# Late stages of a fused attention and gated-MLP gradient kernel: DMAs issued in program order, transposed w_down loaded in chunks, first operands of the next stage loaded into dead buffers

## The chip, the core and the metric

The kernel runs on one core of a Trainium2 chip. The core has five engines with a queue of instructions each: TensorE (PE, matmuls; its weight loads are listed apart as PEld), VectorE (DVE), ScalarE (ACT), GpSimd (POOL) and SyncE (SP). An engine works through its queue in order, and an instruction starts when the semaphores that it waits for have come. DMAs are issued by POOL (plain copies, queue q0 of the profile) and by SP (here mostly DMAs that transpose, queue q1); 16 DMA engines carry them out. SBUF is the working memory, PSUM takes the sums of the matmuls.

The metric is the device time of one execution in microseconds (us), as the median of several runs. Smaller is better.

## What is computed

The kernel computes a block and all its gradients for a given grad_out. S = 2048 rows, D = 576, H = 32 heads of 128, F = 4608, everything in bfloat16:

```python
def _fwd_reference(A_x, A_k_cache, A_v_cache, A_wq, A_wo, B_x, B_w_gate, B_w_up, B_w_down):
    def _A_ref(x, k_cache, v_cache, wq, wo):
        ...
        scores = jnp.einsum("bhqd,bhkd->bhqk", q, k_cache) * (Dh ** -0.5)
        p = _softmax(scores, axis=-1)
        o = jnp.einsum("bhqk,bhkd->bhqd", p, v_cache)
        return (lambda x, *d: x.transpose(*d))(o, 0, 2, 1, 3).reshape(B, Sq, H * Dh) @ wo
    def _B_ref(x, w_gate, w_up, w_down):
        g = jnp.einsum("bsd,df->bsf", x, w_gate)
        u = jnp.einsum("bsd,df->bsf", x, w_up)
        h = _sigmoid(g) * u
        return jnp.einsum("bsf,fd->bsd", h, w_down)
    x = A_x
    xn = _layernorm(x, axis=-1)
    s = _A_ref(xn, A_k_cache, A_v_cache, A_wq, A_wo)
    g = _silu(_B_ref(xn, B_w_gate, B_w_up, B_w_down))
    return x + s * g
```

The outputs are this value (out_0) and the gradients of x (out_1), of the k and v caches (out_2, out_3), of wq (out_4), wo (out_5), w_gate, w_up and w_down (out_6 to out_8).

## The kernel before

The kernel has a forward MLP pass, the attention with its gradients, and then four late stages, which the change touches. A row tile is 128 of the 2048 rows, so there are 16 (`NT`); `DT` = 5 tiles cover the 576 columns and `FT` = 36 the 4608. Some results go through DRAM between stages (names ending in `_d`).

- The forward pass (to about 540 us) ends with loop L403 to L439. For each row tile it computes the MLP's output, and DVE makes from it g2 (the silu), ds_t (grad_out times g2) and dsil, the derivative of silu (L433). g2, dsil and ds_t are stored.
- The attention (to about 3711 us) works head by head and leaves in DRAM `on2_d`, the heads' outputs (shown as on_d), and `dq2_d`, the gradients of the queries (shown as dq_d).
- **Stage A** (L760 to L829): s = o @ wo, row tile by row tile. For each tile, a transposing DMA (`load_oT`, L469) brings the tile's 32 heads into one of two buffers, KQ and oTb, in turn; 32 heads in two column pieces make 64 matmuls (L813). The rows of wo lie in dead buffers of the attention (dsT, Kn, Vn, dOn), except the last six heads, which come in `wo_x`. DVE then makes doB = s * dsil * grad_out (L819, L820), the gradient at the MLP's output, and o0 = s * g2 + x (L822, L823) from loads of two tiles each (L797 to L803, one buffer each). doB is transposed on PE (L58). In the same loop stand loads for stage B: the whole of w_down transposed (wdT_sb, ten pieces, L786), xn_all (L790) and the first blocks of a and h (L792, L793).
- **Stage B** (L854 to L893): 18 blocks of 256 columns of F. A block has 80 matmuls for dh = doB @ w_down^T (L872), DVE and ACT make du and dg of it (L873 to L877), and 3 x 64 matmuls (L842) make the weight gradients. Those of w_up and w_gate are transposed by SP (L892) before they are stored (L850, L852).
- **Stage C** (L908 to L931): for each head 32 matmuls for the gradient of wo (onb by ds_all) and 32 for that of wq (dqb by xn_all). onb and dqb come for four heads at a time (L916, L917), in two buffers each. The gradient of wq leaves through dqT (two buffers, L925) and a transposing DMA by SP (L926). The loop also loads w_up and w_gate transposed, ten pieces (L928 and L63, into wuT_sb and wgT_sb).
- **Stage D** (L938 to L1010): the gradient of the normed x for 8 blocks of 256 rows, each the sum over 36 + 36 + 32 tiles of du @ w_up^T, dg @ w_gate^T and dq @ w_q^T, 416 matmuls (L964). The left operands come as transposed chunks by SP (cu, cg, cq, L955); w_q^T is loaded in five pieces in the first blocks (L957).

What sets the order: the program is written for a framework that puts the instructions of each engine in an order of its own, by its estimate of when they can start, and derives every wait from the tiles that an instruction reads and writes. So a load in the text of stage A can be issued before or after others of the same engine. The late pools are opened by

```python
    def late(name, bufs=1, **kw):
        return tc.tile_pool(name=name, bufs=bufs, reuse_waits="tile", **kw)
```

which makes a new tile wait only for the tiles whose memory it takes.

Of the kernel before, what the change touches and what calls it, by code (L numbers as in the profile page):

```python
# [9 lines left out]
bf = mybir.dt.bfloat16  # L10
# [3 lines left out]
P = 128  # L14
# [52 lines left out]
def kernel(  # L67
# [36 lines left out]
    dsil_d = dram.tile([S, D], bf, name="dsil_d")  # L104
# [126 lines left out]
    with tc.tile_pool(name="pa", bufs=1) as pa:  # L231
# [166 lines left out]
        with tc.tile_pool(name="a2h", bufs=3) as hp, \  # L398
# [4 lines left out]
            for sg in range(NT // SG):  # L403
# [4 lines left out]
                dsil = sb.tile([P, SG, D], bf, name="dsil")  # L408
                g2b = sb.tile([P, SG, D], bf, name="g2b")
                ds_t = sb.tile([P, SG, D], bf, name="ds_t")  # L410
                for sl in range(SG):
# [21 lines left out]
                    nc.vector.tensor_tensor(dsil[:, sl, :], sig[:], t1[:], op=ALU.subtract)  # L433
# [4 lines left out]
                nc.gpsimd.dma_start(dsil_d[grows, :].rearrange("(t p) d -> p t d", p=P), dsil[:])  # L438
# [307 lines left out]
    with late("pc") as pc:  # L746
        xn_all = pc.tile([P, NT, D], bf, name="xn_all")
        pc2 = tc.alloc_tile_pool(name="pc2", bufs=1, reuse_waits="tile")
# [3 lines left out]
        pcw = tc.alloc_tile_pool(name="pcw", bufs=1, reuse_waits="tile")  # L752
        wdT_sb = pcw.tile([P, DT, F], bf, name="wdT_sb")
        pcf = tc.alloc_tile_pool(name="pcf", bufs=1, reuse_waits="tile")
        ah_first = [pcf.tile([P, NT, FB], bf, name=nm) for nm in ("a_first", "h_first")]

        def load_blk(dst, src_d, fb):
            nc.gpsimd.dma_start(dst[:], src_d[:, fb * FB:(fb + 1) * FB].rearrange("(t p) f -> p t f", p=P))

        with late("c1w") as wp, late("c1b") as blk, late("c1l3") as ldp3, late("c1s", 2) as sb, \  # L760
# [14 lines left out]
            WH = ldiv(FT, 2) * P if FT % 2 else F // 2  # L775
            wd_pieces = [(i, r0) for i in range(DT) for r0 in range(0, F, WH)]
            NWD = -(-len(wd_pieces) // max(1, NT - 5))
            pend_tr = []
            for st in range(NT):
                if st + 1 < NT:  # L780
                    load_oT(oTs[(st + 1) % 2], st + 1)
                for _ in range(NWD if st else 0):
                    if wd_pieces:
                        i, r0 = wd_pieces.pop(0)
                        d0 = min(i * P, D - P)
                        nc.sync.dma_start_transpose(wdT_sb[:, i, r0:r0 + WH], B_w_down[r0:r0 + WH, d0:d0 + P])  # L786
                        if not wd_pieces:
                            zlow(wdT_sb)
# [5 lines left out]
                if st % SG1 == 0:  # L794
                    grows = slice(st * P, (st + SG1) * P)
                    g2b = ldp3.tile([P, SG1, D], bf, name="g2b")
                    nc.gpsimd.dma_start(g2b[:], g2_d[grows, :].rearrange("(t p) d -> p t d", p=P))  # L797
                    dsb = ldp3.tile([P, SG1, D], bf, name="dsb")
                    nc.gpsimd.dma_start(dsb[:], dsil_d[grows, :].rearrange("(t p) d -> p t d", p=P))
                    xb = ldp3.tile([P, SG1, D], bf, name="xb")  # L800
                    nc.gpsimd.dma_start(xb[:], x2[grows, :].rearrange("(t p) d -> p t d", p=P))
                    gob = ldp3.tile([P, SG1, D], bf, name="gob")
                    nc.gpsimd.dma_start(gob[:], go2[grows, :].rearrange("(t p) d -> p t d", p=P))  # L803
                    o0b = ldp3.tile([P, SG1, D], bf, name="o0b")
# [19 lines left out]
                if sl == SG1 - 1:  # L824
                    nc.gpsimd.dma_start(o0[grows, :].rearrange("(t p) d -> p t d", p=P), o0b[:])
# [216 lines left out]
```

## Time and profile before

| what | value |
|---|---|
| median of 3 runs | 5245.4 us (5234.62 to 5245.75) |
| the profiled execution's own time | 5251.32 us |
| its span in the trace | 5249.3 us |
| stage A: first matmul, next stage's first | 3720.9, 3916.4 us |
| stage B: first use of xn_all on PE | 3935.5 us |
| stage B to C: last matmul ends, next starts | 4502.0, 4535.5 us |
| stage D: first matmul, ACT starts on the last sum | 4811.7, 5239.4 us |
| L433, dsil: 16 DVE instructions | 749 ns each |
| cu chunks (768 KB), issue to landing | 5.4 us median, 9.0 at most |
| dwT transposes of stage B (L892), issue to landing | 2.4 us (dwg), 6.7 us (dwu) median |

How to read the views: a row of the timeline has the start, the duration in the queue or on the engine, the engine, the line, the operation and out<-in; in square brackets stands how long the engine had been idle before it and what ended that. In the view of waits, "PE acc L842 <- DMA onb<-on_d" means that the matmul of line 842 that writes acc waited for the DMA that loads onb. In the list of DMA issues, the last number is the median time from issue to landing. SPq and POOLq are the issuing queues of those engines. A DMA share of 1 means that the 16 DMA engines were busy all the time on average; more than 1 comes from transfers that overlap on an engine.

### The profile page before, as it was taken

The numbers are of one execution on the slowest core, as the hardware profiler recorded it, in microseconds if no ns is written. First come the engines' busy times: TensorE is split into PE (matmuls) and PEld (weight loads), VectorE is DVE, ScalarE is ACT, GpSimd is POOL, SyncE is SP. The second block draws the span as 40 slices with busy tenths as digits, with TensorE's granted clock in tenths as the row PEclk, the third lists the DMA queues.
The fourth block names the chain that finished last, engine by engine and source line by source line (L and its number), as shares of the span: only waits on it lengthen the run. The fifth ranks groups of instructions, "written<-read, shape, count | busy, mean of one in ns | idle before, by whom it ended". The sixth has DMA issues, their size and how long they took to land.

```text
span 5249.3 us, 127878 instructions
## 1 busy us (share of the span) xinstructions
PE 4959.8 (94%) x53585; PEld 3490.0 (66%) x54480; DVE 2580.0 (49%) x6718; ACT 2600.7 (50%) x4663; POOL 901.3 (17%) x1373
## 2 busy tenths in 40 slices
PE   7899999999999999999999999999689999598999
PEld 3345677777787787777777777777446666354454
DVE  4523566566566666666666666666234444000111
ACT  6421666666676676666666666666113333111000
POOL 1112211111111111111111111111122222111000
PEclk9999999999999999999999999999899999899999
DMA  7647999999999999999999999999976665977775
GB/s 269 228 159 176 188 208 209 206 210 204 193 211 216 201 211 205 202 209 212 201 203 196 210 207 210 209 202 215 218 175 190 179 181 169 220 191 168 157 150 109
DMA packets 2756448, 1033.71 MB, mean 197 GB/s; under 512 B 2662737, under 2 KB 2666962, under 8 KB 2755858
## 3 DMA queue, kind: packets, MB, share of 16 engines
q1 hardware_dynamic: 2658338, 699.96, 72.5%
q0 software_dynamic: 97520, 325.41, 19.3%
q8 instruction: 428, 7.01, 0.6%
q14 instruction: 162, 1.33, 0.1%
HBM read 177.67 MB, written 182.13 MB: 69 GB/s over the span
## 4 chain that ended last, share of the span: by engine, by line
PE 79%; issue 7%; DMA 6%; SPq 3%; DVE 2%; POOL 1%; ACT 1%; POOLq 0%; DVEq 0%; ACTq 0%
PE acc L622 15%; PE acc L563 14%; PE acc L842 12%; PE acc L964 7%; PE sp L516 7%; PE dp L586 5%; PE acc L212 5%; PE dh L872 3%; PE acct L145 2%; PE u_ps L365 2%; PE g_ps L363 2%; PE acc L425 2%; SPq L63 2%; DMA out_dram<-kvo 2%; PE acc L813 1%
## 5 line engine op out<-in xcount | busy, mean ns | idle before, releaser
L534 ACT ACTIVATE Pq<-sp 128x1024 bf16<-128x1024 f32 x1024 | 1048.0, 1024 | 318.5 <-PE sp L516 204.9
L622 PEld LDWEIGHTS <-Pq 128*128 128x128 bf16 x16384 | 1006.1, 98 | 242.3 <-issue 4.4
L593 ACT ACTIVATE t<-dp,negdelta 128x1024 bf16<-128x1024 f32 x512 | 571.6, 1116 | 222.1 <-PE dp L586 168.7
L589 DVE SCALAR_TENSOR_TENSOR Pq<-dp,negdelta,Pq 128x1024 bf16<-128x1024 f32 x512 | 655.6, 1280 | 43.7 <-PE acc L563 40.8
L563 PEld LDWEIGHTS <-PT 128*128 128x128 bf16 x8192 | 502.9, 98 | 129.3 <-DMA PT<-Pq 7.6
L586 PE MATMUL dp<-VT,dOT 128*128 128x512 bf16 x1728 | 543.9, 381 | 35.4 <-DVE Pq L589 35.1
L563 PE MATMUL acc<-Vn,PT 128*128 128x128 bf16 x8192 | 547.7, 219 | 14.0 <-DMA PT<-Pq 7.1
L563 PE MATMUL acc<-Kn,dST 128*128 128x128 bf16 x8192 | 552.1, 219 | 8.2 <-DMA dST<-Pq 4.7
L622 PE MATMUL acc<-dOn,Pq 128*128 128x128 bf16 x8192 | 546.9, 219 | 10.1
L516 PE MATMUL sp<-KQ 128*128 128x512 bf16 x1762 | 548.4, 380 | 2.8 <-ACT Pq L534 2.7
L622 PE MATMUL acc<-Qn,Pq 128*128 128x128 bf16 x8192 | 544.3, 220 | 3.4
L563 PEld LDWEIGHTS <-dST 128*128 128x128 bf16 x8192 | 493.1, 98 | 67.3 <-DMA dST<-Pq 6.6
L594 DVE TENSOR_TENSOR Pq<-t,Pq 128x1024 bf16<-128x1024 bf16 x512 | 354.3, 692 | 357.1 <-ACT t L593 350.4
L980 DVE SCALAR_TENSOR_TENSOR junk<-dxn,xn_all 128x576 f32<-128x576 f32 x16 | 12.1, 758 | 711.9 <-ACT dxn L975 711.9
L603 ACT ACTIVATE dq_n<-acc,rsc 128x128 bf16<-128x128 f32 x512 | 188.3, 368 | 338.3 <-PE acc L563 338.3
L636 POOL DMA_DIRECT2D out_dram<-kvo x256 | 140.2, 548 | 1042.0 <-DVE kvo L634 1036.7
L557 POOL DMA_DIRECT2D on_d<-o_n x128 | 97.0, 758 | 742.7 <-DVE junk L575 392.1
L975 ACT ACTIVATE dxn<-acc 128x512 f32<-128x512 f32 (+1 forms) x32 | 12.8, 407 | 414.7 <-issue 310.1
L363 PE MATMUL g_ps<-wg_sb,xnT 128*128 128x512 bf16 x695 | 184.2, 388 | 28.8 <-DMA wg_sb<-in_B_w_gate_dram 15.0
L634 DVE SCALAR_TENSOR_TENSOR kvo<-acc,part 128x512 bf16<-128x512 f32 x256 | 176.1, 688 | 70.3 <-DMA out_dram<-kvo 35.4
L586 PEld LDWEIGHTS <-dOT 128*128 128x128 bf16 x2048 | 164.0, 98 | 63.2 <-issue 41.1
L50 DVE TENSOR_SCALAR o_n<-acc,rinv_all 128x128 bf16<-128x128 f32 x352 | 123.4, 351 | 168.2 <-PE acc L563 168.2
(199 smaller groups left out, 6842.6 us busy)
## 6 DMA issues: line engine op xcount, KB each, us to landing
out_dram<-kvo POOLq DMA_DIRECT2D x256, 128.0 KB, 4.2
h_d<-h_row POOLq DMA_DIRECT2D x48, 384.0 KB, 2.9
a_d<-a_row POOLq DMA_DIRECT2D x48, 384.0 KB, 2.8
du_d<-du_blk POOLq DMA_DIRECT2D x18, 1024.0 KB, 5.5
dg_d<-dg_blk POOLq DMA_DIRECT2D x18, 1024.0 KB, 7.8
x_all<-in_A_k_cache_dram SPq DMA_DIRECT2D x64, 256.0 KB, 5.6
on_d<-o_n POOLq DMA_DIRECT2D x128, 128.0 KB, 4.1
dq_d<-dq_n POOLq DMA_DIRECT2D x128, 128.0 KB, 3.8
```

The source lines that it names most:

```text
L212: nc.tensor.matmul(av[:, :CH], lhsT=w[:, i, :], rhs=srcT[:, i, cs], start=(i == 0), stop=(i == DT - 1))
L363: nc.tensor.matmul(g_ps[:], lhsT=xnT[:, i, srows], rhs=wg_sb[:, i, fs], start=(i == 0), stop=(i == DT - 1))
L516: nc.tensor.matmul(sp[:, c * CH:(c + 1) * CH], lhsT=hs.QT[:, qt * P:(qt + 1) * P], rhs=hs.KT[:, hf * HW_ + c * CH: hf * HW_ + (c + 1) * CH ...
L534: nc.scalar.activation(Pq[:, hsl], sp[:], AF.Exp, scale=SCALE, accum_out=hs.rsp[:, hf:hf + 1])
L563: nc.tensor.matmul(hs.acc[:, 0, :], lhsT=T[:, kt, :], rhs=rhs[:, kt, :], start=(kt == 0), stop=(kt == NT - 1))
L586: nc.tensor.matmul(dp[:, c * CH:(c + 1) * CH], lhsT=hs.dOT[:, qt * P:(qt + 1) * P], rhs=hs.VT[:, hf * HW_ + c * CH: hf * HW_ + (c + 1) * C ...
L589: nc.vector.scalar_tensor_tensor(Pq[:, hsl], dp[:], hs.negdelta[:, qt:qt + 1], Pq[:, hsl], op0=ALU.add, op1=ALU.mult)
L593: nc.scalar.activation(t[:], dp[:], AF.Identity, bias=hs.negdelta[:, qt:qt + 1], scale=1.0)
L594: nc.vector.tensor_tensor(Pq[:, hsl], t[:], Pq[:, hsl], op=ALU.mult)
L622: nc.tensor.matmul(self.tile[:, j, :], lhsT=self.slabs[qt][:, kt * P:(kt + 1) * P], rhs=self.rhs[:, qt, :], start=(qt == self.lo), stop=(q ...
L842: nc.tensor.matmul(accs[j][:, :nn], lhsT=lhs[:, st, cols], rhs=rhs[:, st, n0:n0 + nn], start=(st == 0), stop=(st == NT - 1))
L964: nc.tensor.matmul(self.accs[sl][j][:, :nn], lhsT=ch[:, kk, sl * P:(sl + 1) * P], rhs=wT[:, k0 + kk, n0:n0 + nn], start=(self.k + kk == 0) ...
```

## The change

What it does, part by part:

1. From stage A on, SP and POOL take their instructions in the order of the program text (`tc.manual_schedule`), and the text places the DMAs accordingly. The other engines are ordered as before.
2. w_down^T is loaded in 30 chunks of 768 rows by 128 columns (192 KB) in place of ten pieces of 2304 rows (576 KB). The five chunks of the first 768 rows are issued in tiles 9 to 13 of stage A, the others in stage B, two a block in its first ten blocks and one a block in the next five. Behind the fifth of each five, POOL zeroes the padding of the 768 columns (before, one memset for all).
3. The product of dsil and grad_out is formed in the forward pass (dsg, one DVE instruction more per row tile there, one fewer in stage A). The load of grad_out in stage A goes. The loads of stage A have two buffers and are issued one group (two tiles) ahead.
4. xn_all is loaded at the start of stage B; the first a and h block from tile 12 of stage A.
5. In the last block of stage B, ds_all, the first onb and the first dqb are loaded into the memory of wdT_sb and of the a/h buffer ah0, which are dead by then. Stage C's dwq lies there too, and later w_q^T of stage D.
6. In stage C the onb/dqb pair of the next four heads is issued at the top of each group. The ten pieces of w_up^T and w_gate^T are issued at heads 1, 3, ... 19. In the last group SP issues the first two chunks of stage D, into ah0.
7. Stage D has four chunk buffers for all its left operands, chunks of dq of 8 tiles (before 16), loads them in the order of use, reads grad_out at the top of a block, and forms the product with xn_all from PSUM in two instructions.

The core of the difference:

```diff
-                    nc.vector.tensor_tensor(dsil[:, sl, :], sig[:], t1[:], op=ALU.subtract)
+                    nc.vector.tensor_tensor(t1[:], sig[:], t1[:], op=ALU.subtract)
+                    nc.vector.tensor_tensor(dsg[:, sl, :], t1[:], got[:, sl, :], op=ALU.mult)
...
-    with late("pc") as pc:
+    with late("pc") as pc, late("pcw") as pcw, late("pcf") as pcf, \
+            tc.manual_schedule(engines={mybir.EngineType.SP, mybir.EngineType.Pool}):
...
+        wd_pieces = [(i, r0) for r0 in range(0, F, WCH) for i in range(DT)]
+        def wd_piece():
+            if wd_pieces:
+                i, r0 = wd_pieces.pop(0)
+                d0 = min(i * P, D - P)
+                nc.sync.dma_start_transpose(wdT_sb[:, i, r0:r0 + WCH], B_w_down[r0:r0 + WCH, d0:d0 + P])
+                if i == DT - 1 and KPAD:
+                    nc.gpsimd.memset(wdT_sb[:LO, i, r0:r0 + WCH], 0.0)
...
-                if st == min(2, NT - 1):
-                    nc.gpsimd.dma_start(xn_all[:], xn_d[:, :].rearrange("(t p) d -> p t d", p=P))
-                if st == NT // 2:
-                    load_blk(ah_first[0], a_d, 0)
-                    load_blk(ah_first[1], h_d, 0)
...
+                if sl == 0:
+                    if g + 1 < NG1:
+                        groups[g + 1] = group_loads(g + 1)
...
+                if st >= NT - 2 - DT and len(wd_pieces) > (F // WCH - 1) * DT:
+                    wd_piece()
+                if st == NT - NT // 4:
+                    load_blk(ah0[:, 0, :, :], a_d, 0)
+                    load_blk(ah0[:, 1, :, :], h_d, 0)
...
+                if fb == 0:
+                    nc.gpsimd.dma_start(xn_all[:], rows_view(xn_d, 0, D))
...
+                for _ in range(-(-len(wd_pieces) // max(1, NFB - fb - WCH // FB))):
+                    wd_piece()
...
+                if fb == NFB - 1:
+                    nc.gpsimd.dma_start(ds_all, rows_view(ds_d, 0, D))
+                    load_heads(onb0, dqb0, 0)
...
+                if hg + 1 < NHG:
+                    load_heads(*onqs[(hg + 1) % 2], hg + 1)
...
-                    if hg >= min(1, H // HG - 1):
-                        wT_piece()
+                    if h % gap == gap - 1 and wT_pieces:
+                        load_T_rows(nc, *wT_pieces.pop(0))
+                    if hg == NHG - 1 and hl < len(cf_pre) and NHG % 2 == 0:
+                        chunks[hl] = load_chunk(hl)
...
-                        nc.vector.scalar_tensor_tensor(junk[:], dxn[:], 1.0, xn_all[:, st, :], op0=ALU.mult, op1=ALU.mult, accum_out=c2[:])
+                            nc.vector.scalar_tensor_tensor(junk[:, n0:n0 + nn], self.accs[sl][j][:, :nn], 1.0, xn_all[:, st, n0:n0 + nn],
+                                                           op0=ALU.mult, op1=ALU.mult, accum_out=cc[:, 1, j:j + 1])
...
+            for n, (sbi, which, k0) in enumerate(seq):
+                if n not in chunks:
+                    chunks[n] = load_chunk(n)
+                if n % 2 and n >= 3 and wq_pieces:
+                    load_T_rows(nc, wqT_sb, A_wq, *wq_pieces.pop(0))
```

How the rows stand on the engines, at three places. First, what SP issues from the end of the attention, before:

```order
L734 UNCONDITIONAL_BRANCH
L786 DMA_TRANSPOSE wdT_sb<-in_B_w_down_dram 128x2304 x2
L470 DMA_TRANSPOSE oTb<-on_d 128x32x128
L470 DMA_TRANSPOSE KQ<-on_d 128x32x128
L786 DMA_TRANSPOSE wdT_sb<-in_B_w_down_dram 128x2304 x5
L470 DMA_TRANSPOSE oTb<-on_d 128x32x128
L786 DMA_TRANSPOSE wdT_sb<-in_B_w_down_dram 128x2304 x2
L470 DMA_TRANSPOSE KQ<-on_d 128x32x128
L786 DMA_TRANSPOSE wdT_sb<-in_B_w_down_dram 128x2304
```

In the change, SP issues ten loads of oTb and KQ first with nothing between them; the end of its rows for stage A and the start of those for stage B are now:

```order
L774 DMA_TRANSPOSE wdT_sb<-in_B_w_down_dram 128x768
L471 DMA_TRANSPOSE KQ<-on_d 128x32x128
L774 DMA_TRANSPOSE wdT_sb<-in_B_w_down_dram 128x768
L471 DMA_TRANSPOSE oTb<-on_d 128x32x128
L774 DMA_TRANSPOSE wdT_sb<-in_B_w_down_dram 128x768 x2
L933 DMA_TRANSPOSE dwu<-dwT_124566 128x5x128
L933 DMA_TRANSPOSE dwu<-dwT_124567 128x5x128
L933 DMA_TRANSPOSE dwg<-dwT_124568 128x5x128
```

The w_down^T loads have moved behind tile 9's oT load, and most of them into stage B ahead of each block's dwT transposes.

Second, what POOL issues from the end of the attention, before:

```order
L734 UNCONDITIONAL_BRANCH
L790 DMA xn_all<-xn_d 128x16x576
L465 DMA wo_x<-in_A_wo_dram 128x6x576
L758 DMA a_first<-a_d 128x16x256
L758 DMA h_first<-h_d 128x16x256
L797 DMA g2b<-g_d 128x2x576
L799 DMA dsb<-dsil_d 128x2x576
```

and with the change (the numbers in the names tell the buffers of the two groups apart):

```order
L735 UNCONDITIONAL_BRANCH
L466 DMA wo_x_123169<-in_A_wo_dram 128x6x576
L799 DMA dsg_123172<-dsg_d_60 128x2x576
L799 DMA g2b_123174<-g2_d_59 128x2x576
L799 DMA xb_123176<-in_A_x_dram 128x2x576
L799 DMA dsg_123179<-dsg_d_60 128x2x576
```

wo_x stands first now; xn_all and the a and h blocks have gone from here, and the second group's loads stand right behind the first's.

Third, the passage from stage B to stage C on SP. Before, where dwu and dwg are the last block's and dwq is stage C's:

```order
L892 DMA_TRANSPOSE dwg<-dwT_124607 128x5x128
L63 DMA_TRANSPOSE wuT_sb<-in_B_w_up_dram 128x36x64
L63 DMA_TRANSPOSE wgT_sb<-in_B_w_gate_dram 128x36x128 x4
L63 DMA_TRANSPOSE wgT_sb<-in_B_w_gate_dram 128x36x64
L926 DMA_TRANSPOSE dwq<-dqT_132054 128x5x128
L926 DMA_TRANSPOSE dwq<-dqT_132055 128x5x128
```

and with the change, where dwq lies in the memory of wdT_sb:

```order
L933 DMA_TRANSPOSE dwg<-dwT_124569 128x5x128
L987 DMA_TRANSPOSE wdT_sb<-dqT_132046 128x5x128
L987 DMA_TRANSPOSE wdT_sb<-dqT_132047 128x5x128
L63 DMA_TRANSPOSE wuT_sb<-in_B_w_up_dram 128x36x128
L987 DMA_TRANSPOSE wdT_sb<-dqT_132046 128x5x128
L987 DMA_TRANSPOSE wdT_sb<-dqT_132047 128x5x128
```

The pieces of w_up^T and w_gate^T no longer stand ahead of the first dwq transposes; one follows each second of them. On POOL, the last block's rows before were

```order
L879 DMA dg_d<-dg_blk 128x16x256
L884 DMA out_dram<-dwd 128x576 x2
L850 DMA out_dram<-dwu 128x4x256
L852 DMA out_dram<-dwu 64x256
L910 DMA ds_all<-ds_d 128x16x576
L850 DMA out_dram<-dwg 128x4x256
```

and are now

```order
L917 DMA dg_d<-dg_blk 128x16x256
L919 DMA wdT_sb<-ds_d 128x16x576
L883 DMA wdT_sb<-on_d 128x16x512
L884 DMA ah_123145<-dq_d 128x16x512
L925 DMA out_dram<-dwd 128x576 x2
```

The loads of ds_all (into wdT_sb) and of the first onb and dqb moved ahead of the last block's stores.

More of the change, by code (lines that the diff above doesn't have):

```diff
@@ new lines, with add @@
+        HC = ldiv(H, FC)
+        cf_n = FC * SB2
+        ah0_flat = ah0[:].rearrange("p a t f -> p (a t f)")
+        cf_pre = [ah0_flat[:, k * cf_n:(k + 1) * cf_n] for k in range(2 * NT * FB // cf_n)]
+        fu, fg, fq = (du_d, FT, FC), (dg_d, FT, FC), (dq2_d, H, HC)
+        seq = []
+        def add(sbi, which):
+            seq.extend((sbi, which, k0) for k0 in range(0, which[1], which[2]))
+        NB2 = min(2, NSB)
+        for which in (fu, fg):
+            for sbi in range(NB2):
+                add(sbi, which)
@@ L968, in finish @@
                 def finish(self):
+                    nj = len(ncs)
                     for sl in range(nsl):
@@ L993, in finish @@
                         nc.gpsimd.dma_start(o1[rows, :], dx[:])
-            fg = ((du_d, wuT_sb, FT, FC, "cu"), (dg_d, wgT_sb, FT, FC, "cg"))
-            fq = ((dq2_d, wqT_sb, H, HC, "cq"),)
-            NB2 = min(2, NSB)
-            first = [Rows(sbi) for sbi in range(NB2)]
-            for r in first:
-                r.passes(fg)
-            while wq_pieces:
-                load_T_rows(nc, wqT_sb, A_wq, *wq_pieces.pop(0))
-            for r in first:
-                r.passes(fq)
-                r.finish()
```

216 lines of the change are left out of this document (116 added, 100 removed).

## The prediction

> **What bounds the kernel now.** I read the busy times of the page first. TensorE (PE) is busy 94% of the span, so time can only be won where PE waits:
>
> ```profile
> PE 4959.8 (94%) x53585; PEld 3490.0 (66%) x54480; DVE 2580.0 (49%) x6718; ACT 2600.7 (50%) x4663; POOL 901.3 (17%) x1373
> ```
>
> Then the view of waits, for PE after the attention stage (from 3711 us), longest first; the columns are total, times and longest:
>
> ```profile
> PE acc L842 <- DMA onb<-on_d: 33.5, 1, 33.5
> PE acc L813 <- DMA oTb<-on_d: 25.3, 5, 19.6
> PE acc L842 <- ACT dqT L40: 20.9, 1, 20.9
> PE acc L813 <- DMA wo_x<-in_A_wo_dram: 19.4, 1, 19.4
> ```
>
> All four are waits for data, early in stages A and C. The 20.9 us charged to ACT are a DMA wait too: ACT could not reuse dqT, because the transposes that empty it stood behind five w_gate pieces in SP's queue. These are SP's rows (start, duration in the queue); dwq comes only at 4590.14:
>
> ```profile
> 4520.58 69.30 SPq L63 DMA_TRANSPOSE wgT_sb<-in_B_w_gate_dram  x5
> 4590.14 214.57 SPq L926 DMA_TRANSPOSE dwq<-dqT  x31
> ```
>
> Next, the late part cut by stages: length, busy time of PE, PEld, DVE, ACT, POOL, then clock, DMA share and GB/s:
>
> ```profile
> 3720.90:3916.40 195.50, 137.51 (x1076) 71.52 (x1099) 42.37 (x60) 18.95 (x44) 35.72 (x44) 0.87 0.93 197
> 3916.40:3951.30 34.90, 33.21 (x279) 20.48 (x282) 22.46 (x68) 11.42 (x30) 9.11 (x13) 1.00 0.66 202
> 3951.30:4502.10 550.80, 547.17 (x4557) 338.95 (x4622) 243.51 (x800) 174.27 (x477) 138.41 (x166) 1.00 0.62 175
> 4502.10:4535.50 33.40, 0.00 (x0) 0.00 (x0) 0.00 (x0) 0.64 (x2) 7.45 (x10) 0.53 1.13 292
> 4535.50:4572.60 37.10, 36.39 (x282) 18.77 (x289) 0.00 (x0) 3.50 (x10) 4.01 (x5) 0.96 1.15 267
> 4572.60:4593.50 20.90, 0.03 (x2) 0.00 (x0) 0.00 (x0) 0.62 (x3) 0.00 (x0) 0.57 1.14 149
> 4593.50:4810.60 217.10, 215.24 (x1725) 111.31 (x1759) 0.00 (x0) 39.55 (x115) 37.95 (x54) 0.99 0.65 172
> 4810.60:4951.10 140.50, 122.84 (x957) 62.66 (x978) 12.59 (x32) 4.27 (x18) 6.68 (x12) 0.96 0.92 185
> 4951.10:5239.40 288.30, 285.81 (x2307) 148.14 (x2352) 34.36 (x88) 9.83 (x44) 10.74 (x20) 1.00 0.65 132
> ```
>
> Stage A is the first row, B the next two, C four, D the last two. PE at its own pace does 32 matmuls (one accumulation of stage C) in 3.92 us, the step between the last two of these rows; the first, behind a wait, runs at a lower clock and takes 1.3 us more:
>
> ```profile
> 4593.51 5.39 PE L842 MATMUL acc<-xn_all,dqb 128*128 128x512 bf16 x31 [20.88 <-ACT dqT L40]
> 4598.74 4.08 PE L842 MATMUL acc<-ds_all,onb 128*128 128x512 bf16 x32
> 4602.66 4.08 PE L842 MATMUL acc<-xn_all,dqb 128*128 128x512 bf16 x31
> ```
>
> So a matmul is worth 0.1225 us, and each stage has a floor. A: 16 tiles of 64 matmuls and about 0.3 us of transposes, 8.1 us each, 130 us; it takes 195.5, 65.5 over. B: 32.4 us a block (550.8/17); only the first block is 2.5 over. C: 64 accumulations, 251 us; from 4502.1 to 4810.6 are 308.5, 57.6 over. D: 3,328 matmuls, 408 us; to 5239.4 are 428.8, 21 over. The change can win at most these 147 us.
>
> **Stage A.** It loses the ten w_down^T pieces that stood between the oT loads, xn_all and the first a/h block ahead of wo_x, and gob. Five of the pieces alone held SP's queue for
>
> ```profile
> 3756.60 25.64 SPq L786 DMA_TRANSPOSE wdT_sb<-in_B_w_down_dram  x5
> ```
>
> The landing times (KB each, median us from issue to landing) of before are
>
> ```profile
> wo_x<-in_A_wo_dram POOLq DMA_DIRECT2D x1, 864.0 KB, 20.5
> ...
> oTb<-on_d SPq DMA_TRANSPOSE x8, 9.5
> KQ<-on_d SPq DMA_TRANSPOSE x7, 8.5
> ```
>
> wo_x is now first on POOL and shares the engines with one oT load. No row shows it so; bounds are 5.5 us (du_d, 1024 KB, quoted below) and 20.5; I take 7, near the first, since the 2.3 MB ahead of it and the pieces beside it are gone. Issued at 3725 as xn_all was, it lands at about 3732, and tile 0 ends at 3735 (12 matmuls at the low clock), and KQ's next load, issued then, lets tile 2 start at 3744. From there two buffers set the pace: a load can start only when its buffer's tile is done, so two tiles take 8.1 us plus the landing. With 9.3 us (oTb's 9.5, a little less since the group loads shrink from five transfers to four) a tile costs 8.7. The late tiles of before, which had no piece beside them, agree: from
>
> ```profile
> 3845.11 4.33 PE L813 MATMUL acc<-dsT,KQ 128*128 128x512 bf16 x33
> ```
>
> to 3916.4 eight tiles took 8.9 each. Fourteen tiles give 122 us; the a/h block at tile 12 and five small w_down^T chunks I put at 4. Stage A ends near 3870: **46 us won**. Bounds: 60 (loads fully hidden, 15 x 8.1 from 3735) and 31 (wo_x at 3740, a/h costing 10). The DVE product that goes shortens a chain that ends beside PE's next tile: 0.
>
> **The product moved into the forward pass** costs 16 DVE instructions of 0.75 us. There DVE has room beside a full PE (a 20 us stretch, same columns):
>
> ```profile
> 420.00:440.00 20.00, 19.84 (x168) 10.60 (x170) 8.26 (x13) 2.01 (x5) 6.27 (x8) 1.00 0.82 204
> ```
>
> Cost 0; without that cover it would be 12 us.
>
> **Stage B.** The 25 chunks left are transposes on SP, two a block, ahead of the four dwT transposes. A chunk is 192 KB; by the 5.0 us of a w_up piece of 1152 KB (row below) it holds SP for 0.8 us, 1.7 us in a block whose DMA share is 0.62. Behind it wait only the dwT transposes, which feed stores and have four buffers; cost 0. Every fifth chunk puts a memset on POOL that waits for its landing; behind it stand the du_d and dg_d stores, which nothing reads in this stage. xn_all is now issued about 4 us after PE leaves stage A (behind the last o0b store) and is needed 19 us after (its first use before was at 3935.5). By ds_all's 11.1 us (same size) it lands at 15, by wo_x's 20.5 in the crowd at 24.5: I take 0, by ds_all, with bounds of 0 and 5 lost. The a/h loads of each next block now stand behind the last dwg store:
>
> ```profile
> a_next<-a_d POOLq DMA_DIRECT2D x8, 1024.0 KB, 9.6
> ```
>
> ```profile
> L873 DVE SCALAR_TENSOR_TENSOR nbl<-a_next,h_next x144: 417/422/429, 3933.9 to 4452.3; 128x256 bf16<-128x256 bf16 x144
> ```
>
> Issued some 6 us into a block, the pair lands by about 17; DVE's 16 nbl products (0.42 us each) must start by 25.7. Hidden, 8 us to spare.
>
> **Into stage C.** In a block of stage B the du_d store goes out 10.6 us after PE began it:
>
> ```profile
> 4113.17 9.05 PE L872 MATMUL dh<-wdT_sb,doBT 128*128 128x256 bf16 x80
> ...
> 4123.81 1.20 POOL L878 DMA_DIRECT2D du_d<-du_blk  x1 [5.47 <-DVE nbl L873]
> ```
>
> In the last block dg_d, ds_all, onb0 and dqb0 now follow at 1.2 us each, all issued by 16.6, and PE needs onb0 at 32.4:
>
> ```profile
> onb<-on_d POOLq DMA_DIRECT2D x8, 2048.0 KB, 9.5
> dqb<-dq_d POOLq DMA_DIRECT2D x8, 2048.0 KB, 17.5
> ...
> ds_all<-ds_d POOLq DMA_DIRECT2D x1, 2304.0 KB, 11.1
> du_d<-du_blk POOLq DMA_DIRECT2D x1, 1024.0 KB, 5.5
> dg_d<-dg_blk POOLq DMA_DIRECT2D x1, 1024.0 KB, 9.0
> ```
>
> They run one behind the other. dg_d lands near 20; 4.5 MB of ds_all and onb0 at 200 to 292 GB/s (the stage rows) end at 35 to 42, dqb0's 2.1 MB at 42 to 52, 3.9 us after which PE wants it. Waits of 6 to 16 us remain where 33.4 were; I take 10, and 1.3 for the clock. The ten w_up/w_gate pieces now go out one per two heads, heads 1 to 19, each behind two dwq transposes, so the 20.9 us wait goes. What is late next is the DMA itself: five groups of four heads (31.4 us) carry 4.2 MB of loads, 2.4 MB of pieces and 1.8 MB of dwq, dwo and out_4: 8.4 MB. At 249 GB/s, the mean of the three crowded rows of stage C, that is 33.7 us, 2.3 too long; half of it is absorbed by the loads' head start. I take 5 for all; bounds 0 and 25. Left over 16 of 57.6: **42 us won**, bounds 18 and 51.
>
> How loads and pieces share matters here. A piece of w_up went out beside light traffic, one of w_gate beside the onb/dqb loads (ns, min/median/max):
>
> ```profile
> L63 SPq DMA_TRANSPOSE wuT_sb<-in_B_w_up_dram x5: 4791/4986/5639, 4486.4 to 4515.5; - x5
> ...
> L63 SPq DMA_TRANSPOSE wgT_sb<-in_B_w_gate_dram x5: 2467/13512/25964, 4520.6 to 4587.4; - x5
> ```
>
> The piece gave way (5 to 26 us), the load did not. The Trainium skill ("DMA: Bandwidth & Descriptors", section "Queues, rings and completion order") says that each DMA engine takes turns between queues, a packet at a time. By that rule loads and pieces would halve each other's pace, and the onb/dqb pair would come late in each of the five groups: the first rival below. The trace speaks against equal halves.
>
> **Stage D.** Two chunks are loaded in C's last group and cover 11.8 us of PE. Chunk 3 is issued when stage C's last store has landed, some 2 us into D, and lands by 10. After that two chunks and a w_q piece per 11.8 us of PE fill SP about as full as it was. I leave 3 of the 21 us: **18 won**, bounds 11 and 21. The end of the kernel stays: the new DVE product still waits for ACT's read of the same sum.
>
> **Sum.** 46 + 0 + 42 + 18 = 106 us off the profiled execution's 5251.3 us: 5145. The median of the runs is 5.9 us below that execution, so 5139; I say 5140.
>
> **Rivals.** (1) DMA saturates in stage C: for is the share of 1.13 to 1.15 in all crowded rows, against is the GB/s still free there. If the five groups go at 200 GB/s, 42 us each, they lose 53 instead of 5 and the other groups win it back nowhere: 5188. (2) The change does not do what it says in stage A: wo_x and the first oT load come late for their own reasons (attention's last stores), and only the pieces' waits go. Then A wins about 25: 5161. For it: the pace of 8.9 us needs no piece; against it: wo_x waited behind 2.3 MB. (3) Slower: POOL's program order makes the a/h loads late in stage B. Each of 17 blocks would lose what the pair lands after 25.7 us. It cancels the 106 us when it lands at 32, 15 us later than worked out; at 35, 158 are lost: 5298. Against it: nothing ahead of these loads waits longer than the dwT transposes, 2 to 7 us.
>
> **How the numbers follow.** Forecast 0.70 (5114 to 5160), rival 1 0.15, rival 2 0.11, rival 3 0.04. Faster by over 0.2% (10 us, about what a measurement can tell from no change) has 0.95, same 0.01, slower 0.04. The parts' worst and best ends together would give 55 to 133 us; not all fall on one side, so I go from 71 to 131 won, half of rival 1 included: 5114 to 5174.
>
> **What would show it.** Right: PE's wait for wo_x under 8 us, stage A at 150 us, no wait on dqT's ACT copy, an onb wait of 6 to 16 us and 255 to 275 us for stage C, D at 408 to 415. Wrong: waits on onb or dqb in groups 2 to 6 (rival 1), oT waits over 1.5 us a tile (rival 2), nbl or dh waiting for ah0/ah1 in every block (rival 3).

## The result, and the profile after

| what | before | changed kernel |
|---|---|---|
| median of 4 runs | 5240.0 us (5230.8 to 5245.8) | 5124.6 us (5118.7 to 5125.6) |
| ratio | | 0.9779 (95% interval 0.9760 to 0.9798) |
| the profiled execution's own time | 5251.3 us | 5124.0 us |
| stage A | 195.5 us | 146.8 us |
| stage B | 585.7 us | 582.7 us |
| stage C, from the end of B's last matmul | 308.5 us | 255.7 us |
| stage D, from the end of C's last matmul to ACT's start on the last sum | 428.8 us | 412.7 us |
| tail | 9.9 us | 10.8 us |
| sum of these five | 1528.4 us | 1408.7 us |
| start of stage A in the trace | 3720.9 us | 3713.5 us |

Where PE waits at most 0.5 us between stages B and C, as in the changed kernel, the tables count this wait in B.

The late part is 119.7 us shorter. The remaining 7.4 us of the difference between the two traces lie ahead of stage A, where only the 16 small products are new; in the fourteen profiled executions of this study stage A starts anywhere from 3705.8 to 3727.4 us, so these 7.4 us are scatter of the executions and not the change. A stage's length of the same code repeats better: 255.4 to 255.7 us for stage C, 582.4 to 582.8 for B, 143.3 to 148.6 for A, 409.7 to 412.7 for D.

The busy time of the engines first, then the late part in stretches (length; busy time of PE, PEld, DVE, ACT, POOL; granted clock, DMA share, GB/s). Stage A, stage B, the first five groups of stage C, its last three, stage D, the tail:

```profile
PE 4944.7 (97%) x53585; PEld 3482.8 (68%) x54480; DVE 2585.3 (50%) x6734; ACT 2600.0 (51%) x4663; POOL 895.8 (17%) x1370
```

```profile
3713.50:3860.30 146.80, 134.31 (x1078) 70.52 (x1101) 32.76 (x45) 19.06 (x45) 25.72 (x35) 0.97 0.89 201
3860.30:4443.00 582.70, 578.07 (x4831) 359.26 (x4900) 268.23 (x867) 187.19 (x507) 155.42 (x188) 1.00 0.64 194
4443.00:4474.40 31.40, 28.19 (x212) 14.33 (x218) 0.00 (x0) 4.50 (x14) 6.78 (x11) 0.95 0.99 271
4474.40:4505.80 31.40, 31.14 (x253) 16.13 (x256) 0.00 (x0) 5.50 (x16) 5.83 (x8) 1.00 0.92 264
4505.80:4537.20 31.40, 31.14 (x253) 16.13 (x256) 0.00 (x0) 5.50 (x16) 5.84 (x8) 1.00 0.93 265
4537.20:4568.60 31.40, 31.14 (x254) 16.17 (x258) 0.00 (x0) 5.50 (x16) 5.83 (x8) 1.00 0.87 248
4568.60:4600.00 31.40, 31.14 (x254) 16.17 (x258) 0.00 (x0) 5.51 (x16) 5.83 (x8) 1.00 0.97 270
4600.00:4698.70 98.70, 97.86 (x793) 50.74 (x808) 0.00 (x0) 17.41 (x50) 15.70 (x23) 1.00 0.60 173
4698.70:5111.40 412.70, 406.34 (x3263) 210.99 (x3328) 46.45 (x132) 14.11 (x63) 17.47 (x32) 1.00 0.84 153
5111.40:5122.20 10.80, 0.00 (x0) 0.00 (x0) 5.30 (x12) 0.87 (x4) 1.09 (x2) 0.74 0.08 27
```

PE is full in every one of these groups of stage C but the first, while the DMAs move 248 to 271 GB/s beside it. The view of waits, for PE from the end of the attention on (total, times, longest), has none of the four long waits left:

```profile
PE acc L826 <- DMA oTb<-on_d: 4.4, 3, 3.6
PE acc L826 <- DMA KQ<-on_d: 3.4, 1, 3.4
PE acc L855 <- DMA ah<-dq_d: 2.9, 1, 2.9
PE acc L1026 <- DMA cf<-du_d: 2.8, 2, 2.2
PE acc L826 <- DMA out_dram<-kvo: 2.6, 1, 2.6
PE pt L58 <- DVE doB L831: 2.0, 2, 1.6
PE acc L826 <- DMA wo_x<-in_A_wo_dram: 1.6, 1, 1.6
PE acc L855 <- DMA wdT_sb<-on_d: 0.4, 1, 0.4
```

The waits of stage C's first operands are the rows of wdT_sb (onb0 lies there) and ah (dqb0): 0.4 and 2.9 us where onb alone cost 33.5. The 20.9 us behind dqT are gone.

### The profile page after: what moved, and what is told of

It is laid out like the page before. It is cut to its first block, busy times and chain, and to the rows that moved or that the text cites. A ratio compares the mean times of both kernels' runs of the same rounds, so it can differ in the third digit from the quotient of the medians.

```text
span 5122.2 us, 127940 instructions
## 1 busy us (share of the span) xinstructions
PE 4944.7 (97%) x53585; PEld 3482.8 (68%) x54480; DVE 2585.3 (50%) x6734; ACT 2600.0 (51%) x4663; POOL 895.8 (17%) x1370
## 4 chain that ended last, share of the span: by engine, by line
PE 80%; issue 9%; DMA 6%; DVE 2%; POOL 1%; ACT 1%; SPq 0%; POOLq 0%; DVEq 0%; ACTq 0%
PE acc L623 15%; PE acc L564 15%; PE acc L855 12%; PE sp L517 7%; PE acc L1026 7%; PE acc L212 5%; PE dp L587 5%; PE dh L908 3%; PE acct L145 2%; PE u_ps L365 2%; PE g_ps L363 2%; DMA out_dram<-kvo 2%; PE acc L425 2%; PE acc L826 2%; DMA x_all<-in_A_k_cache_dram 1%
## 5 line engine op out<-in xcount | busy, mean ns | idle before, releaser
L623 PE MATMUL acc<-dOn,Pq 128*128 128x128 bf16 x8192 | 546.2, 219 | 10.1
L1042 DVE SCALAR_TENSOR_TENSOR junk<-acc,xn_all 128x512 f32<-128x512 f32 (+1 forms) x32 | 13.9, 452 | 641.7 <-ACT dxn L1041 641.7
L910 DVE TENSOR_TENSOR du_blk<-dh,ah 128x256 bf16<-128x256 f32 x288 | 120.3, 418 | 190.3 <-PE dh L908 188.2
L522 DVE TENSOR_REDUCE rs_all<-rsp 128x1 f32<-128x2 f32 x512 | 78.1, 152 | 256.3 <-ACT Pq L535 254.1
```

What stands on the lines that cost most here:

```text
L623: nc.tensor.matmul(self.tile[:, j, :], lhsT=self.slabs[qt][:, kt * P:(kt + 1) * P], rhs=self.rhs[:, qt, :], start=(qt == self.lo), stop=(q ...
```

## The experiments

All are edits of the changed kernel; each has a profile of one execution. The table has the stages as above (us); "sum" is the five together, to be held against 1408.7 and, in a second execution of the changed kernel, 1408.2. "Time" is that one execution, in the last three rows the median of 5. The 7.2 us that the run "a/h later" waits for onb0 are counted in B. Since executions scatter ahead of stage A, the verdicts go by these stages.

| run | A | B | C | D | tail | sum | time |
|---|---|---|---|---|---|---|---|
| no program order | 202.0 | 586.3 | 288.7 | 416.3 | 9.5 | 1502.8 | 5221.1 |
| w_down chunks early | 185.1 | 582.8 | 255.6 | 411.8 | 10.8 | 1446.1 | 5168.1 |
| xn_all ahead of wo_x | 153.1 | 582.7 | 255.5 | 409.7 | 10.8 | 1411.8 | 5134.9 |
| stage C's operands late | 148.6 | 582.5 | 273.7 | 412.3 | 11.5 | 1428.6 | 5158.8 |
| all pieces first | 144.1 | 582.5 | 295.8 | 412.6 | 10.8 | 1445.8 | 5155.1 |
| pieces dense | 143.3 | 582.8 | 265.0 | 409.8 | 10.8 | 1411.7 | 5128.7 |
| no chunks ahead | 146.0 | 582.4 | 254.2 | 421.9 | 10.8 | 1415.3 | 5123.0 |
| a/h late | 146.8 | 620.5 | 255.7 | 411.6 | 11.2 | 1445.8 | 5168.8 |
| a/h later | 147.0 | 699.7 | 253.8 | 411.2 | 10.6 | 1522.3 | 5239.0 |
| changed kernel again | 147.3 | 582.8 | 255.4 | 411.9 | 10.8 | 1408.2 | 5126.1 |
| combination | 143.7 | 582.2 | 250.8 | 408.4 | 10.6 | 1395.7 | 5116.2 |
| combination 2 | 134.7 | 582.2 | 250.9 | 410.3 | 10.6 | 1388.7 | 5109.8 |

### The order alone

```diff
-    with late("pc") as pc, late("pcw") as pcw, late("pcf") as pcf, \
-            tc.manual_schedule(engines={mybir.EngineType.SP, mybir.EngineType.Pool}):
+    with late("pc") as pc, late("pcw") as pcw, late("pcf") as pcf:
```

> The changed kernel without the program order for SP and POOL; buffers, chunks and preloads stay. SP then has 22 of the 30 w_down chunks among its first two oT loads, POOL has xn_all ahead of wo_x and ds_all behind the first onb and dqb, and the w_up/w_gate pieces go out in pairs ahead of the first dwq transposes. Theory (the order wins the time): stage A 25 to 50 us longer than the 147 of the changed kernel, stage C 10 to 40 longer than 256, 5160 to 5210 in all. Rival (the smaller chunks and the dead buffers win it, the order matters little): within 10 us of 5124.

Measured: 5221 us, 94 us lost of the 120 that the late part had won; stage A 202 us, 6 more than in the kernel before, and stage C 33 more than in the changed kernel. Stage A lies past the theory's bound of 50 us more, stage C inside its 10 to 40, and the total 11 us past 5210; the rival is far off. SP's rows of this run (start, duration in the queue) show how:

```profile
3745.16 4.68 SPq L471 DMA_TRANSPOSE oTb<-on_d  x1
3749.89 24.54 SPq L773 DMA_TRANSPOSE wdT_sb<-in_B_w_down_dram  x18
3774.54 9.29 SPq L471 DMA_TRANSPOSE oTb<-on_d  x1
3783.88 15.65 SPq L773 DMA_TRANSPOSE wdT_sb<-in_B_w_down_dram  x8
```

The 18 chunks cost SP as much as five of the old pieces did, and PE waited 44.7 us in all for oTb. Smaller chunks and dead buffers are worth little without the order; they are what lets the order be written.

### Stage A: what stood in SP's and POOL's queues

```diff
-                if st >= NT - 2 - DT and len(wd_pieces) > (F // WCH - 1) * DT:
-                    wd_piece()
+                if st < 5:
+                    for _ in range(6):
+                        wd_piece()
...
-            while len(wd_pieces) > (F // WCH - 1) * DT:
-                wd_piece()
```

> The 30 w_down chunks go out six behind each of the first five oT loads of stage A, in place of five late in stage A and 25 in stage B. Theory (what stage A lost in the kernel before was SP's queue): each next oT load comes about 4 us late, 15 to 25 us more of oT waits in tiles 2 to 7, stage A 162 to 172 us. Rival (the oT waits of before came from the plain loads beside them): within 5 us of 147.

Measured: stage A 185.1 us, 38 lost, more than the 15 to 25 expected. The waits stand where the theory has them (oTb 24.6 us in 3, KQ 10.8 in 4), but I had taken a chunk at 1.3 us; six took 7.9 us alone and up to 18.1 us beside the plain loads, and one oT load took 12.4.

```diff
+            nc.gpsimd.dma_start(xn_all[:], rows_view(xn_d, 0, D))
             wo_of = {}
...
-                if fb == 0:
-                    nc.gpsimd.dma_start(xn_all[:], rows_view(xn_d, 0, D))
```

> xn_all (2.3 MB) is loaded ahead of wo_x on POOL, as before the change. Theory (wo_x was late because it stood behind 2.3 MB): wo_x lands about 8 us later and PE waits 8 to 13 us for it in place of 1.6; stage A 155 to 160. Rival (wo_x was late because of the transposing pieces beside it, or by itself): at most 3 us more.

Measured: wo_x landed 11.3 us after its issue, not 6.1, PE waited 9.4 us for it in place of 1.6, and stage A took 153.1 us. The wait is the one expected, the stage 2 us shorter than expected. So 2.3 MB ahead of wo_x explain 5 of the 14 us by which it was late before. The other 9 stay open: the pieces beside it are the obvious candidate, but in the run with the chunks early, six of them in SP's queue beside it, wo_x landed in 6.8 us.

### Stage C: early operands, and the pieces

```diff
-                if fb == NFB - 1:
-                    nc.gpsimd.dma_start(ds_all, rows_view(ds_d, 0, D))
-                    load_heads(onb0, dqb0, 0)
...
             gap = max(1, (H - HG) // len(wT_pieces))
+            nc.gpsimd.dma_start(ds_all, rows_view(ds_d, 0, D))
+            load_heads(onb0, dqb0, 0)
```

> ds_all, onb0 and dqb0 are issued at the top of stage C, behind the last stores of stage B, in place of in its last block. Theory (the preload wins stage C's first wait): PE waits 25 to 35 us for onb at the start of stage C, all else as it was, about 5155. Rival (the loads would have landed anyway, the wait of before came from the w_gate pieces beside them): a wait under 15 us.

Measured: a wait of 20.7 us, between the two: 18.0 us lost in stage C. What made it 33.5 before is seen on POOL, before and in this run, around the end of stage B's last matmul (4502.0 and 4458.4 us):

```profile
4521.27 0.77 POOL L850 DMA_DIRECT2D out_dram<-dwg  x1 [11.45 <-DMA dwg<-dwT]
...
4522.74 1.19 POOL L916 DMA_DIRECT2D onb<-on_d  x1
```

```profile
4462.53 0.79 POOL L863 DMA_DIRECT2D out_dram<-dwg  x1 [6.95 <-issue]
...
4465.22 1.17 POOL L883 DMA_DIRECT2D wdT_sb<-on_d  x1
```

In both, POOL reaches the load of onb only behind the store of dwg, which needs SP's transposes (the second view names no releaser; SP issued the last of these transposes at 4459.1 us). Before, they stood behind pieces of w_up^T and landed in 8.1 to 9.8 us, here in 2.1 to 4.0; onb was issued 20.7 us after the last matmul, here 6.8. The rest, 13 to 14 us, is the landing. By these rows the pieces had a share of up to 13 us in the longest wait too, by way of a store; no run adds the pieces alone to this one.

```diff
             gap = max(1, (H - HG) // len(wT_pieces))
+            while wT_pieces:
+                load_T_rows(nc, *wT_pieces.pop(0))
```

> All ten pieces of w_up^T and w_gate^T stand ahead of stage C's first dwq transpose on SP, the loads of onb and dqb as in the changed kernel. Theory (a queue delay on SP): the pieces hold SP for 50 to 75 us, dwq waits behind them, and PE waits 30 to 50 us behind the ACT copy into dqT, with onb and dqb waits under 5 us: about 5165. Rival (equal sharing of the DMA engines): the second group's onb and dqb come late, with PE waits on them over 10 us.

Measured: the pieces hold SP for 77.7 us, stage C takes 40 us more, nearly all of it in two waits behind ACT's copies:

```profile
PE acc L855 <- ACT dqT L40: 20.9, 1, 20.9
PE acc L855 <- ACT dwo L40: 15.1, 1, 15.1
```

The first is the theory's: ACT waits for the buffer dqT, dqT for SP's dwq transposes, and these stand behind the pieces. It is as long as in the kernel before, 20.9 us. The second, 15.1 us, comes from late loads, as the rival has it, although PE's view names ACT. These are ACT's row and the landing of the stores that it waited for:

```profile
4484.90 1.31 ACT L40 CAST dwo<-acc 128x512 bf16<-128x512 f32 x4 [29.43 <-DMA out_dram<-dwo]
```

```profile
out_dram<-dwo POOLq DMA_DIRECT2D x2, 144.0 KB, 29.7
```

ACT could not reuse dwo until its stores had landed, 29.7 us after POOL issued them right behind the loads of the second group; onb took 29.6 us to land and dqb 30.5 (9.4 and 13.5 in the changed kernel). PE was free for onb at 4470.5 us and onb landed at 4475.3, so PE would have waited for the loads themselves without this. Of the 40 us, 20.9 are the theory's queue and 15.1 go with the rival's late loads.

```diff
-            gap = max(1, (H - HG) // len(wT_pieces))
+            gap = 1
```

> One w_up/w_gate piece per head, heads 0 to 9, in place of one per two heads: groups 1 and 2 ask for about 10.6 MB in 31.4 us (338 GB/s) each. Theory (the plain loads take what they need, the pieces give way): onb lands in 9 to 12 us and dqb in 13 to 17 as before, pieces take 7 to 10 us in SP's queue, at most 8 us lost, in dqT waits: 5124 to 5132. Rival (DMA saturates near the 270 GB/s seen): 8 us lost in each of the two groups, in onb or dqb waits: about 5140.

Measured: 9 us lost in stage C, where the theory has at most 8; the time lies inside its 5124 to 5132 because stage A was 3.5 us shorter in this execution. onb landed in 9.3 to 11.3 us and dqb in 14.0 to 16.7, no later than in the changed kernel. A piece that went out behind a pair of loads stayed in SP's queue for 15.1 to 17.8 us, the others for 4.6 to 6.3 (the half piece 3.0):

```profile
4485.16 1.24 SPq L987 DMA_TRANSPOSE wdT_sb<-dqT  x1
4486.45 5.47 SPq L63 DMA_TRANSPOSE wuT_sb<-in_B_w_up_dram  x1
4492.01 1.23 SPq L987 DMA_TRANSPOSE wdT_sb<-dqT  x1
4493.30 15.11 SPq L63 DMA_TRANSPOSE wuT_sb<-in_B_w_up_dram  x1
```

The loss came as 7.1 us behind ACT's copy into dwo, not into dqT: SP's dwq came late behind the slow piece, POOL's store of dwq waited for it, and behind that on POOL stand the next pair of loads and then the dwo stores, which took 16.0 us to land. While loads and a piece share the engines, the packets of the two queues (q0 the loads, q1 the transposes; packets, MB, share of 16 engines) are, in this run from 4494 to 4504 us and in the kernel before from 4536 to 4546:

```profile
q0 software_dynamic: 822, 3.18, 95.3%
q1 hardware_dynamic: 588, 0.14, 9.4%
```

```profile
q0 software_dynamic: 939, 3.78, 94.7%
q1 hardware_dynamic: 939, 0.24, 10.6%
```

The counts of packets are of the same order, but a packet of a load has about 4 KB and one of a transpose 0.25 KB. So the loads move 16 to 23 times the bytes and keep 95% of the engines' time.

### Stage D and stage B

```diff
-                    if hg == NHG - 1 and hl < len(cf_pre) and NHG % 2 == 0:
+                    if hg == NHG - 1 and hl < 0:
```

> The first two chunks of stage D are not loaded in stage C's last group; the rest of stage D as in the changed kernel. Theory (the preload wins a part of stage D, the order of use the rest): 7 to 11 us more, all of it in waits on the first chunks: about 5133. Rival (the order and the four shared buffers win it): at most 3 us more.

Measured: PE waits 11.1 us for the first chunk, and stages C and D together take 676.1 us, 7.7 and 8.8 more than in the two executions of the changed kernel: the theory's size. (The time doesn't show it, since stage A began 7.7 us earlier in this execution.) About half of stage D's gain of 16.1 us is left for the order of use and the four shared buffers; that half wasn't undone by itself.

Two runs move the a/h loads of the next block down: in the first behind the dwd stores, in the second behind the dwu stores.

```diff
-                if fb + 1 < NFB:
-                    nxt = (ah0, ah1)[(fb + 1) % 2]
-                    load_blk(nxt[:, 0, :, :], a_d, fb + 1)
-                    load_blk(nxt[:, 1, :, :], h_d, fb + 1)
...
                     nc.gpsimd.dma_start(out_8[r0:r0 + P, :], dwd[:])
+                if fb + 1 < NFB:
+                    nxt = (ah0, ah1)[(fb + 1) % 2]
+                    load_blk(nxt[:, 0, :, :], a_d, fb + 1)
+                    load_blk(nxt[:, 1, :, :], h_d, fb + 1)
```

> In stage B the a/h loads of the next block are issued behind the block's two dwd stores, some 18 us into a block of 32.2, not 5. Theory (by the prediction's third rival: DVE's 16 nbl products need 5.5 to 6.7 us before the next block, so a landing later than about 26 us into the block is lost one for one): the pair lands at 26 to 30, 0 to 4 us lost in each of 17 blocks, 20 to 60 in all. Rival (DVE and the four dh buffers absorb it): under 5 us in all.

> As the run before, but the a/h loads stand behind the dwu stores, some 29 us into the block. By the prediction's third rival the pair lands at 37 to 41 and each of 17 blocks loses that less 26: 11 to 15 us a block, 190 to 255 us in all, about 5340. Rival (part of it is absorbed by DVE's free time in the next block, since only the first dh tiles need the first products): under 130 us.

Measured: stage B 37.8 us longer (2.2 a block) in the first, and 117.0 in the second, of them 7.2 in a wait for onb0 and 6.5 a block for the rest. The first agrees with the theory, the second with its rival: the price isn't one for one. In the first, the pair lands 31.3 us into a block:

```profile
4148.20 5.46 DVE L905 SCALAR_TENSOR_TENSOR nbl<-ah 128x256 bf16<-128x256 bf16 x16 [18.85 <-DMA ah<-h_d]
...
4150.87 2.35 PE L904 MATMUL dh<-wdT_sb,doBT 128*128 128x256 bf16 x20
4154.52 6.93 PE L904 MATMUL dh<-wdT_sb,doBT 128*128 128x256 bf16 x60 [1.30 <-ACT ndh L908]
```

A landing at 31.3, less the 25.7 of the rule, would cost 5.6. It costs less, for two reasons that the rows show: the 16 products take 5.46 us (0.34 each, not 0.42), and with four dh buffers PE does 20 matmuls of the next block before it needs DVE. In the second the pair lands about 46 us into the block, and the framework has interleaved the dwd matmuls and the nbl products with the dh tiles, which hides more.

### What was left, taken together

The combination adds four edits: a third oT buffer in the memory of xn_all, which is loaded only in stage B; dqb0, ds_all and onb0 issued ahead of the last du and dg stores; two more chunks of stage D in onb0; and the product with xn_all from SBUF as before.

```diff
-            oTs = [oT0 if ... , blk.tile([P, H, P], bf, name="oTb")[:]]
+            oTs = [oT0 if ... , blk.tile([P, H, P], bf, name="oTb")[:], xn_oT]
...
-                if st + 1 < NT:
-                    load_oT(oTs[(st + 1) % 2], st + 1)
+                for n in ([1, 2] if st == 0 else [st + 2]):
+                    if n < NT:
+                        load_oT(oTs[n % 3], n)
...
+                if fb == NFB - 1:
+                    nc.gpsimd.dma_start(dqb0, rows_view(dq2_d, 0, HG * P))
+                    nc.gpsimd.dma_start(ds_all, rows_view(ds_d, 0, D))
+                    nc.gpsimd.dma_start(onb0, rows_view(on2_d, 0, HG * P))
                 nc.gpsimd.dma_start(rows_view(du_d, fb * FB, FB), du_blk[:])
...
```

> The changed kernel once more, on the chip of the next run: 5118 to 5126, to compare the next run with.

> The changed kernel with four more edits: a third oT buffer in the memory of xn_all (dead in stage A), stage C's first operands ahead of the last du/dg stores, two more chunks of stage D preloaded into onb0, and the product with xn_all from SBUF again. Theory (what is left in the late stages is waits for data): stage A 6 to 12 us shorter, stage C 3 to 5, stage D 1 to 3, the tail 1: 5105 to 5113. Rival (stage A's rest is the pace of PE and the low clock after a wait, and earlier loads collide with stores): within 5 us of the changed kernel.

Measured: 5116.2 us against 5126.1 of the changed kernel (5 runs each; ratios to the kernel before 0.9758, 0.9739 to 0.9777, and 0.9771, 0.9751 to 0.9792: the intervals overlap). That is 3 us past the theory's 5105 to 5113, and further from the changed kernel than the rival's 5. By the stages: C 4.6 to 4.9 shorter, the theory's size; D 3.5 to 4.3, but only 1.3 below the shortest stage D of the same code; A only 3, within its scatter. No oT wait was left there, but a new one had taken its place:

```profile
3733.55 0.64 PE L828 MATMUL acc<-wo_x,KQ 128*128 128x512 bf16 x2 [6.94 <-DMA wo_x<-in_A_wo_dram]
...
3738.62 6.26 PE L828 MATMUL acc<-dsT,oTb 128*128 128x512 bf16 x34
```

Two oT loads in flight put the landing of wo_x to 11.6 us, and behind the wait a stretch of 34 matmuls that takes 4.33 us elsewhere took 6.26. The second combination lets the third buffer come in a tile later:

```diff
-                for n in ([1, 2] if st == 0 else [st + 2]):
+                for n in ([1] if st == 0 else [2, 3] if st == 1 else [st + 2]):
```

> The combination of the run before, but the third oT buffer comes in one tile later, so that only one transposing oT load runs beside wo_x. Theory (in the combination the second oT load in flight is what put wo_x's landing from 6.1 to 11.6 us): wo_x lands in 6 to 7 us, PE waits under 2.5 us for it, no oT waits, stage A 136 to 140 us, the four late stages and the tail 1388 to 1393 us. Rival (wo_x's landing is scatter): the wait stays at 5 us or more and stage A at 142 or more.

Measured: wo_x 6.0 us, the wait 1.8, no oT wait, stage A 134.7 us, 12 less than in the changed kernel, and the five stages 1388.7, 20 less:

```profile
3722.90:3857.60 134.70, 130.03 (x1078) 69.42 (x1101) 32.78 (x45) 19.03 (x45) 25.72 (x35) 0.99 0.94 219
```

Its median is 5109.8 us (5098.5 to 5116.8; ratio 0.9746, 0.9722 to 0.9771), the lowest of the study, though its interval too overlaps that of the changed kernel. Stage A carries the reading: 134.7 us is 8.6 below the shortest of the same code.

## Why the prediction held, and where its sizes were off

Predicted were 5140 us and 106 us won; measured are 5124.6 us, and 119.7 us won in the parts that the sum speaks of.

- **Stage A: 46 predicted, 48.7 measured, with two terms off in opposite directions.** wo_x landed 6.1 us after its issue (7 taken) and PE waited 1.6 us for it. The pace was put too slow: the oT loads landed in 8.3 to 8.6 us (medians), not 9.3, so that a tile without a wait took 8.1 us where I had 8.7, some 8 us over 14 tiles. That the late tiles of before took 8.9 was no property of two buffers. The a/h block cost twice the 4 us put down for it and the chunks: beside it two oT loads landed 11.9 and 17.2 us after their issue (the second was in SP's queue for 14.46), PE waited 3.6 and 3.4 us, and the matmuls behind the first wait took 1.7 us longer, 8.7 in all, inside the bound of 10 (in the second execution it was one wait of 9.1). That the sum came within 3 us is in part luck. Rival 2 fell with wo_x's 6.1 us.
- **The product in the forward pass: 0.** The first matmul of the attention that needs P^T came at 548.0 us, before at 546.8; over the executions of the changed code it is 546.2 to 551.5, so nothing can be told from no change.
- **Stage B: 0 predicted, 3.0 measured**, no wait is left. The a/h pair landed 17.7 us into a block, as worked out. The pair isn't late, so rival 3 didn't come about, and its price was too high: a pair that lands 5.6 us past the point it named costs 2.2 us a block, not 5.6.
- **Stage C: 42 predicted, 52.8 measured, just past its upper bound of 51.** (By the terms that the prediction names, the bounds come to 15 and 50; 52.8 lies outside either way.) Two terms were mis-sized. The wait on the first operands was put at 10 us, with 1.3 for the clock; it was 0.4 and 2.9, with 1.7 more in the first accumulation behind it (5.77 us, later 4.08). I let ds_all, onb0 and dqb0 run at 200 to 292 GB/s, the rates of before's stretches; the DMA moved 329 to 334 while they ran:

```profile
4424.00:4437.00 13.00, 12.89 (x105) 6.73 (x106) 0.00 (x0) 2.10 (x6) 3.04 (x4) 1.00 1.00 334
4437.00:4450.00 13.00, 9.59 (x76) 4.80 (x76) 0.00 (x0) 2.10 (x6) 0.00 (x0) 1.00 1.11 329
```

The rates of before were means over long rows, and its trace had more to show: the stretch below, inside the row of 267 GB/s, moved 402 beside a busy PE and a piece of w_gate^T, while transposes alone moved 231 from 4521 to 4524 us.

```profile
4536.00:4546.00 10.00, 9.54 (x70) 4.78 (x71) 0.00 (x0) 1.40 (x4) 1.72 (x2) 0.89 1.05 402
```

The other term, 5 us for five crowded groups, was 0: no wait on onb or dqb is left in groups 2 to 6. I took the 249 GB/s of before's crowded rows for what the DMA can do; in the changed kernel the same engines moved 264 to 271 GB/s in four of the five groups, with PE full in all but the first. The 8.4 MB of a group in 31.4 us are 267 GB/s, so they moved what was asked. A mean rate seen beside a long queue of transposes is what that mix moved, not a ceiling for another mix. Rival 1 rested on it, and fell with it.
- **Stage D: 18 predicted, 16.1 measured**, 412.7 us inside the 408 to 415 named. **The tail: 0 predicted, 0.9 lost.** The prediction had the end of the kernel stay as it was. But DVE ended 5.55 us after ACT's start on the last sum, before 4.14: the sums of the two last row tiles come 1.96 us apart, before 3.92, since the last chunk has 8 tiles of dq in place of 16, so DVE works on both in turns. The product in two instructions is the smaller part: with one again, in the combination, DVE ended after 5.35.
- **How loads and pieces share.** That the piece gives way held where the loads were already under way (the dense pieces: loads as ever, pieces 15 to 18 us). That the load did not was too strong: before's first onb, beside the w_gate pieces, took 12.7 us to land where the median is 9.5, and where five pieces stood in the queue first the loads gave way (29.6 and 30.5 us). My use of the Trainium skill ("DMA: Bandwidth & Descriptors", section "Queues, rings and completion order") was wrong: turns by the packet don't halve both paces, since the packets are of different size. Counted in the profile's packets, some shared stretches agree with the rule (939 to 939 above, 567 to 569 in the changed kernel from 4437 to 4443 us), others don't (822 to 588 above, and 254 of loads to 747 of transposes in the kernel before from 4547 to 4551 us). What stays open is the run with all pieces first: from 4447 to 4456 us it has 225 packets of loads and 2313 of transposes, with a load of 2 MB waiting. By equal turns that load would have gone through; no run here tells why it didn't.

## What to carry to other kernels

Read the queue of the issuing engine before the engine that the wait names: of the 120 us won here, 94 were lost again when the order in which SP and POOL issue their DMAs was given up, and the waits named onb, oT, dqT and wo_x. Where two queues compete, ask what is ahead in each and what waits behind it, stores included. After each such repair look for what is late next: the third buffer was worth 3 us, no more than the scatter, until the load that it delayed was let through, and 12 then. And look inside a long row before taking its mean rate for a limit.

## What was not expected of the hardware

- Plain loads of 2 MB ran at 329 to 344 GB/s (344 in the run with dense pieces, 4531 to 4545 us, with PE busy for 9.4 of the 14), where the stage rows of the kernel before had shown 292 at most; a stretch of 10 us inside them shows 402.
- A transposing DMA beside plain loads can take three times as long in SP's queue (an oT load 14.46 or 16.39 us in place of 4.7 to 5), but it also slows a small load: wo_x, 864 KB, landed in 6.1 us beside one oT load and in 11.6 beside two.
- A full DMA share says little of the rate: in the run with all pieces first, the engines were busy from 4446 to 4466 us (share 1.24 to 1.30) and moved 152 to 156 GB/s, from 4476 to 4485 (1.27) only 126; in the changed kernel 264 to 271 went with shares of 0.92 to 0.99.
